# Channel attention with a squared-ReLU feed-forward: q's first loads on a second queue, W's low terms and v's split in another order, the last block stored in three pieces

## The chip, the cores and the metric

One core of one Trainium2 chip runs the kernel. The metric is the device time of one execution in microseconds (us), taken as the median of the runs shown; less is better. One execution was also recorded by the hardware profiler, and all rows below are of that execution.

## What is computed

Four batches of q, k and v (6080 tokens x 256 channels, f32) go through attention over the channels, and the result, read as 24320 tokens of 256 channels, through a feed-forward layer:

```python
qn = q / (norm(q, axis=1) + 1e-6);  kn = k / (norm(k, axis=1) + 1e-6)
s = kn.T @ qn / tau                      # 256 x 256 per batch
a = softmax(s, axis=-1)
x = (v @ a).reshape(24320, 256)
h = maximum(x @ w_in, 0)                 # 2048 wide
return (h * h) @ w_out
```

w_in and w_out come as 64-bit floats. The kernel gets v and gives the output with the channels first.

## The kernel before, in words

**What is multiplied.** The kernel never forms x. For each batch it makes a matrix W from a and w_in (256 x 2048), and then for each block of tokens h = relu(v W), and the output from h squared and w_out. All big products are made from two halves of 32 bits that TensorE takes in one pass: a value is split into `hi` and `lo`, and a product is three terms, hi by hi, lo by hi and hi by lo. A batch has 12 blocks of tokens, ten of 512 and two of 480; a block has 16 steps f of 128 hidden channels. One step is a first product (L579: six matmuls into a `ps_h` bank, then ScalarE's Relu into `x`), and two steps later a second product (L629) into `ps_o`. Between them, once for each pair of steps, ScalarE squares `x` (L603), copies it to `g_hi`, and VectorE makes `g_lo` (L616). Most blocks use a scheme with seven products in place of eight for a pair (L651), the first two blocks and the very last one the plain eight (L707).

**The start (batch 0).** `start_first` (L310) walks over the 25 chunks of q and k: 23 of two rows for each partition, one of a single row, one of the last 64 tokens. `load(c)` asks for a chunk nine ahead, k and q as one DMA each of 256 KB, all from the SP queue (L267, L268); chunk 0 is asked for in two halves. Before these the SP queue asks for `tau` (L106), and ScalarE runs one small `first` activation (L113). TensorE multiplies each chunk into `gram` in plain f32, ScalarE squares it, VectorE adds the squares to `acc`. `LAST = 1` chunk is left for later: its products come from `rest` (L347), after the sums of squares.

**From the gram matrix to W.** `softmax_and_W` (L407) is a generator that the loop at L771 moves on, one yield at a time; `beside_first` (L758) names what is put between. In order: the sums of squares over the partitions (`ps_n`), a chain of small VectorE operations to `nr`, the matrices `diag` and `s`, `ps_b`, the softmax, the transposes `ps_t`, the halves of its transpose `eT_hi` and `eT_lo`, and W's products `ps_w`. For group g of 512 columns of W, `products(h, terms)` makes for half h term 0 (wi_hi by eT_hi), term 1 (wi_hi by eT_lo) and term 2 (wi_lo by eT_hi); `evict(h)` copies `ps_w` to `w_hi` (ScalarE) and `w_lo` (VectorE). Meanwhile TensorE makes gram products of the next batch from its first `HEAD = 6` chunks ("heads", plain f32, L355); the other chunks of batches 1 to 3 are split and multiplied with three terms beside the steps (L384).

**The first steps.** The loop at L798 goes over the steps. In the first 32 of them (two blocks, group by group) other work is put between by hand: `stages` (L778) moves on the decoding of the weights from 64-bit floats (item 2 becomes w_in's group 1 with `wi_hi` and `wi_lo`, and so on), `steps_of_W` (L782) names the steps 6, 14 and 22 in which the next group of W is made, and `split_v_lo` (L566) makes `v_lo` of the second block in step 1, after the step's stages. Every instruction of TensorE, VectorE and ScalarE is kept in the order in which it is written (L19), so all of these have the line L27 in the profile.

**The end.** The last block's two halves m of the output lie in one `ps_o` tile of two banks. The last step does the matmuls of m = 0 first (L717). Then ScalarE copies m = 0 and VectorE m = 1 into one tile `o`, and each half is stored from the SP queue (L741).

Of the kernel before, what the change touches and what calls it, by code (L numbers as in the profile page):

```python
# [8 lines left out]
F32 = mybir.dt.float32  # L9
# [21 lines left out]
def kernel(  # L31
# [21 lines left out]
    nc = tc.nc  # L53
# [12 lines left out]
    J = 2  # L66
    NPAIR = NF // 2
    PPG = FPG // 2
    LAST = 1


    NB = -(-N // T)
# [30 lines left out]
    ones = const.tile([P, P], F32, name="ones")  # L103
    vector.memset(ones, 1.0)
    tau_sb = const.tile([P, 1], F32, name="tau_sb")
    nc.sync.dma_start(tau_sb, tau.to_broadcast([P, 1]))  # L106

    exp_bias = const.tile([P, 1], F32, name="exp_bias")
    vector.memset(exp_bias, -896.0 * 2.0**23)

    for _ in range(7):
        tensor.matmul(ps_h.tile([P, T], F32, tag="h", name="ps_first")[:, 0:P], ones, ones, start=True, stop=True)
    scalar.activation(const.tile([P, 1], F32, name="first"), exp_bias, AF.Square)  # L113
    wo_hi = const.tile([P, NF, C], F32R, name="wo_hi")
    wo_lo = const.tile([P, NF, C], F32R, name="wo_lo")
    late = {}
# [119 lines left out]

    W = {}
    now = {"part": 0}
    HEAD = 6
    QK_BUFS = 2  # L240
    FAST_TAGS = ("qk",) * QK_BUFS + ("w_lo",) * NG + ("w_hi",) * NG

    class Gram:
# [14 lines left out]
        def load(self, c, tag="qk", raw=None):  # L258
            p, jn, _ = self.q[c]
            if raw is None:  # L260
                at = pool if tag == "qk" else wpool
                bufs = dict(bufs=QK_BUFS) if tag == "qk" else {}
                raw = at.tile([P, 2, J, C], F32, tag=tag, name=f"qk{self.b}_{c}", **bufs)

            pieces = [(j, j + 1) for j in range(jn)] if self.b == 0 and c == 0 else [(0, jn)]
            for j0, j1 in pieces:
                nc.sync.dma_start(raw[:p, 1, j0:j1, :], self.k[c][2][:, j0:j1, :])  # L267
                nc.sync.dma_start(raw[:p, 0, j0:j1, :], self.q[c][2][:, j0:j1, :])  # L268
            self.raws[c] = raw

        def products(self, c, parts):
# [38 lines left out]
    def start_first(b=0):  # L310

        g = grams[0] = Gram(0)
        total = g.n + HEAD
        AHEAD = len(FAST_TAGS) - 1

        ROOM = 4
        room = pool.tile([P, ROOM, 2, J, C], F32, tag="wS_lo", name="qk_heads", bufs=1)

        def load(c):
            if c == g.n:  # L320
                grams[1] = Gram(1)
            if c < g.n:
                g.load(c, FAST_TAGS[c % len(FAST_TAGS)])
            elif c < total and B > 1:
                grams[1].load(c - g.n, raw=room[:, c - g.n] if c - g.n < ROOM else None)

        for c in range(AHEAD):
            load(c)
        for c in range(g.n):
            if c < g.n - LAST:  # L330
                for _ in g.products(c, [(g.raws[c], g.raws[c])]):
                    pass
            g.squares(c)
            if c:
                g.add_squares(c - 1)
            load(c + AHEAD)
            if c in (2, 15):
                weights.load(int(c > 2))
            if c in (13, 14, 15, 17):
                weights.stage(0)  # L340
            if c == 19:
                load_v(*order[0])
        for c in range(g.n + AHEAD, total):
            load(c)
        g.add_squares(g.n - 1)

        def rest():  # L347
            for c in range(g.n - LAST, g.n):
                for _ in g.products(c, [(g.raws[c], g.raws[c])]):
                    pass  # L350
            yield

        return rest()
# [53 lines left out]
    def softmax_and_W(b):  # L407
# [81 lines left out]
        for g in range(NG):  # L489
            while (b, g) not in may_write_W:  # L490
                yield
            if b == 0:
                while g not in wi_first:
                    yield
                hi, lo = wi_first.pop(g)
                keep_w_in(g, (hi, lo))
            else:
                hi, lo = wi.pop(g)
            w_hi = wpool.tile([P, NC, GRP], F32R, tag="w_hi", name=f"w_hi{b}_{g}")
            w_lo = wpool.tile([P, NC, GRP], F32R, tag="w_lo", name=f"w_lo{b}_{g}")  # L500
            ps_w = {}

            def products(h, terms=range(3)):
                if h not in ps_w:
                    ps_w[h] = ps_h.tile([P, T], F32, tag="h", name=f"ps_w{b}_{g}_{h}")
                for i in terms:
                    et, wt = ((eT_hi, hi), (eT_lo, hi), (eT_hi, lo))[i]
                    for d in range(NC):
                        tensor.matmul(
                            ps_w[h][:, 0:GRP],  # L510
                            et[:, d, h * P : (h + 1) * P],
                            wt[:, d, :],
                            start=i == 0 and d == 0,
                            stop=i == 2 and d == NC - 1,
                        )

            def evict(h):
                ps = ps_w.pop(h)[:, 0:GRP]
                scalar.activation(w_hi[:, h, :], ps, AF.Copy, scale=rinv[:, h : h + 1])
                vector.scalar_tensor_tensor(  # L520
                    w_lo[:, h, :],
                    ps,
                    rinv[:, h : h + 1],
                    w_hi[:, h, :].bitcast(F32),
                    op0=ALU.mult,
                    op1=ALU.subtract,
                )

            if b == 0:
                for h, terms in ((0, (0, 1)), (1, (0,)), (0, (2,)), (1, (1, 2))):  # L530
                    products(h, terms)
                yield
                for h in range(NC):
                    evict(h)
            else:
                for h in range(NC):
                    products(h)
                    if h == NC - 1 and g + 1 < NG:
                        wi[g + 1] = reload_w_in(b, g + 1)
                    yield  # L540
                    evict(h)
                    yield
            W[b, g] = w_hi, w_lo
            yield
# [162 lines left out]
    def eight_products(b, n, r, part):  # L707
        t0, tn = blocks[n]
        f = 2 * r + part
        if f == 0:  # L710
            O[b, n] = ps_acc.tile([P, NC, T], F32, tag="o", name=f"ps_o{b}_{n}")
        hi, lo = (x.rearrange("p s t -> p (s t)")[:, part * tn : (part + 1) * tn] for x in G[b, n, r])
        parts = ((wo_hi, hi), (wo_lo, hi), (wo_hi, lo))
        order_of = [(i, m) for i in range(3) for m in range(NC)]
        last = (b, n, f) == steps[-1]
        if last:
            order_of.sort(key=lambda im: im[1])  # L717
        for i, m in order_of:
            wt, gt = parts[i]
            tensor.matmul(  # L720
                O[b, n][:, m, :tn],
                wt[:, f, m * P : (m + 1) * P],
                gt,
                start=f == 0 and i == 0,
                stop=f == NF - 1 and i == 2,
            )
        if part:
            del G[b, n, r]
        if f == NF - 1:
            o = pool.tile([P, NC, tn], F32, tag="o_sb", name=f"o{b}_{n}", bufs=1)  # L730
            at = b * N + t0
            out = outT[:, at : at + tn].rearrange("(m p) t -> p m t", p=P)
            psum = O.pop((b, n))
            for m in range(NC):
                ps = psum[:, m, :]
                if last and m:
                    vector.tensor_copy(o[:, m, :], ps[:, :tn])
                else:
                    scalar.copy(o[:, m, :], ps[:, :tn])
                if last:  # L740
                    nc.sync.dma_start(out[:, m : m + 1, :], o[:, m : m + 1, :])  # L741
            if not last:
                nc.sync.dma_start(out, o)

    steps = [(0, n, g * FPG + f) for g in range(NG) for n in range(min(2, NB)) for f in range(FPG)]
    PAIR = len(steps)
# [10 lines left out]

    beside_first = {  # L758
        1: (lambda: next(rest), stage(1), lambda: load_v(*order[1], "acc")),
        5: (head, head, head, head, stage(0), stage(1)),  # L760
        6: (lambda: split_v_hi(*order[0]),),
        8: (head, head, head, head),
        9: (stage(0),),
# [34 lines left out]
    for i in range(len(steps) + 2 * LAG):  # L798
# [8 lines left out]
        if i >= PAIR:  # L807
            gens = (beside,)
        else:
            for item in stages.get(i, ()):  # L810
                weights.stage(item)
            if i == 1:
                split_v_lo(*order[1])
            gens = (first,) if i in steps_of_W else ()
            if i >= 16 and (i >= 24 or part == 0):
                gens += (squares_of_heads if B > 1 and grams[1].raws else sums,)
# [5 lines left out]
                next(gen, None)  # L822
        if part == 0 and 0 <= i // 2 - 1 < len(pairs):
            parts_of_sums(*pairs[i // 2 - 1])
        if i in steps_of_W:
            next(first)
        if part == 1 and i // 2 < len(pairs):
            squares_and_sums(*pairs[i // 2])
        if part and late_work:
# [4 lines left out]
                pass  # L834
        if i >= 2 * LAG:
            second_product(*pairs[i // 2 - LAG], part)
        if i < len(steps):
            at_hi, at_lo = (None, None) if at == 0 else (12, 13) if at == 1 else (6, 8)
            if i == 2 and len(order) > 2:
# [37 lines left out]
```

## Time and profile before

| what | us |
|---|---|
| median of 3 runs | 2215.76 (2215.72 to 2216.32) |
| the profiled execution, its own time | 2216.45 |
| its span on the core | 2214.6 |
| TensorE busy in the span | 2206.4 |
| ScalarE busy | 1842.3 |
| VectorE busy | 1759.8 |

The span is what the rows show, from the first instruction to the last; the execution's own time is 1.85 us more, and lies 0.69 us above the median of the runs. PE is TensorE's matmuls, PEld its weight loads, which run beside the matmuls; DVE is VectorE, ACT ScalarE, SPq the queue that issues DMAs. An f32 matmul shows as two records. In the timeline a row has its start and its length in us, then engine, line, operation, out<-in, the shape, how many are merged (x), and in brackets the idle time before it with what ended it.

### The profile page before, as it was taken

What the parts mean: (1) busy time and instruction counts of PE and PEld (TensorE: products, weight loads), DVE (VectorE), ACT (ScalarE), POOL (GpSimd) and SP (SyncE); (2) the same over time, 40 slices, a digit from 0 to 9 for tenths busy, and PEclk for the clock granted to TensorE, in tenths of its full rate; (3) what the DMA queues carried; (4) which work ended last, traced back from release to release, by engine and by line L of the source; (5) the groups of instructions that cost most, each with busy time, mean ns of one, the idle gap of its engine ahead of it and who ended that gap; (6) DMA issues with size and microseconds to landing.
All of it is one profiled execution on the core that took longest, in us unless ns stands there. A gap on an engine that the chain in (4) does not pass through costs nothing.

```text
span 2214.6 us, 34388 instructions
## 1 busy us (share of the span) xinstructions
PE 2206.4 (100%) x13750; PEld 1982.2 (90%) x13750; DVE 1759.8 (79%) x2469; ACT 1842.3 (83%) x2294; POOL 0.7 (0%) x6
## 2 busy tenths in 40 slices
PE   9999999999999999999999999999999999999999
PEld 8788999989989999998998999998899888888898
DVE  6878888888778888878767888888877777777773
ACT  5788888888788888888878888888887888888885
POOL 0000000000000000000000000000000000000000
PEclk9999999999999999999999999999999999999999
DMA  9521122101111122110121222110102010010000
GB/s 342 179 77 38 60 75 67 46 19 38 57 67 58 61 70 70 55 41 22 36 76 48 69 64 69 58 53 23 37 20 76 21 37 20 22 36 20 22 26 18
DMA packets 76496, 127.01 MB, mean 57 GB/s; under 512 B 7728, under 2 KB 35120, under 8 KB 76336
## 3 DMA queue, kind: packets, MB, share of 16 engines
q1 hardware_dynamic: 76336, 124.81, 17.3%
q8 instruction: 108, 1.77, 0.3%
q14 instruction: 52, 0.43, 0.1%
HBM read 95.68 MB, written 29.10 MB: 56 GB/s over the span
## 4 chain that ended last, share of the span: by engine, by line
PE 98%; DVE 1%; DMA 0%; ACT 0%; issue 0%; SPq 0%; DVEq 0%
PE ps_h L27 47%; PE ps_o L27 43%; PE gram L27 6%; PE ps_w L27 2%; DVE dec_m L27 0%; DMA qk<-in_q 0%; DMA w_raw<-in_w_in 0%; PE ps_n L27 0%; DVE wi_lo L27 0%; ACT x L27 0%; ACT g_hi L27 0%; DVE w_lo L27 0%; PE ps_t L27 0%; PE ps_b L27 0%; DVE g_lo L27 0%
## 5 line engine op out<-in xcount | busy, mean ns | idle before, releaser
L27 DVE TENSOR_TENSOR g_lo<-x,g_hi 128x768 fp32r<-128x768 f32 (+2 forms) x744 | 804.2, 1081 | 97.2 <-ACT g_hi L27 96.5
L27 DVE TENSOR_TENSOR x<-x 128x256 f32<-128x256 f32 (+3 forms) x1080 | 550.8, 510 | 274.5 <-ACT x L27 249.1
L27 ACT CAST g_hi<-x 128x768 fp32r<-128x768 f32 (+2 forms) x744 | 697.8, 938 | 25.0 <-DVE x L27 12.2
L27 ACT ACTIVATE x<-ps_h 128x512 f32<-128x512 f32 (+1 forms) x768 | 455.7, 593 | 289.7 <-PE ps_h L27 266.0
L27 PE MATMUL ps_h<-v_hi,w_hi 128*128 128x512 f32 (+1 forms) x1536 | 478.5, 393 | 0.0
L27 PE MATMUL ps_h<-v_hi,w_lo 128*128 128x512 f32 (+1 forms) x1536 | 477.8, 392 | 0.0
L27 PE MATMUL ps_h<-v_lo,w_hi 128*128 128x512 f32 (+1 forms) x1536 | 475.0, 390 | 0.8 <-DVE v_lo L27 0.8
L27 ACT ACTIVATE x<-x 128x1024 f32<-128x1024 f32 (+1 forms) x384 | 404.4, 1053 | 11.9
L27 PE MATMUL ps_o<-g_lo,wS_hi 128*128 128x256 f32 (+1 forms) x1440 | 401.9, 279 | 0.0
L27 PE MATMUL ps_o<-g_hi,wS_lo 128*128 128x256 f32 (+1 forms) x1440 | 401.2, 279 | 0.0
L27 PE MATMUL ps_o<-g_hi,wS_hi 128*128 128x256 f32 (+1 forms) x1440 | 400.4, 278 | 0.0
L27 PEld LDWEIGHTS ps_h<-v_lo,w_hi 128*128 128x128 f32 x1536 | 287.8, 187 | 65.9 <-DVE v_lo L27 1.2
L27 PEld LDWEIGHTS ps_h<-v_hi,w_lo 128*128 128x128 f32 x1536 | 288.5, 188 | 62.4 <-DVE w_lo L27 0.3
L27 PE MATMUL ps_o<-g_hi,wo_hi 128*128 128x256 f32 (+3 forms) x1176 | 330.9, 288 | 0.0
L27 PE MATMUL ps_o<-g_hi,wo_lo 128*128 128x256 f32 (+3 forms) x1176 | 330.7, 288 | 0.0
L27 PE MATMUL ps_o<-g_lo,wo_hi 128*128 128x256 f32 (+3 forms) x1176 | 330.5, 288 | 0.0
L27 PEld LDWEIGHTS ps_o<-g_lo,wS_hi 128*128 128x128 f32 x1440 | 271.0, 188 | 15.9 <-DVE g_lo L27 0.2
L27 PEld LDWEIGHTS ps_o<-g_hi,wS_hi 128*128 128x128 f32 x1440 | 270.3, 188 | 15.5
L27 PEld LDWEIGHTS ps_o<-g_hi,wS_lo 128*128 128x128 f32 x1440 | 270.6, 188 | 0.0
L27 PEld LDWEIGHTS ps_h<-v_hi,w_hi 128*128 128x128 f32 x1536 | 238.9, 188 | 5.3
L27 PEld LDWEIGHTS ps_o<-g_hi,wo_hi 128*128 128x128 f32 x1176 | 221.5, 188 | 16.4
L27 PEld LDWEIGHTS ps_o<-g_lo,wo_hi 128*128 128x128 f32 x1176 | 220.8, 188 | 16.6 <-DVE g_lo L27 0.3
(90 smaller groups left out, 1668.1 us busy)
## 6 DMA issues: line engine op xcount, KB each, us to landing
qk<-in_k SPq DMA_DIRECT2D x87, 256.0 KB, 2.7
qk<-in_q SPq DMA_DIRECT2D x87, 256.0 KB, 3.0
v<-in_vT SPq DMA_DIRECT2D x40, 512.0 KB, 3.7
out_T<-o SPq DMA_DIRECT2D x152, 128.0 KB, 1.7
wi_hi<-wi_kept SPq DMA_DIRECT2D x12, 512.0 KB, 3.3
wi_lo<-wi_kept SPq DMA_DIRECT2D x12, 512.0 KB, 4.1
w_raw<-in_w_in SPq DMA_DIRECT2D x4, 1024.0 KB, 5.7
w_raw<-in_w_out SPq DMA_DIRECT2D x4, 1024.0 KB, 5.2
```

The costliest lines, as they stand in the source:

```text
L27: return lambda *args, **kwargs: self.tc.keep_in_program_order(issue(*args, **kwargs))
```

## The change

- q's pieces of chunks 0 to 3 of batch 0 are asked for from ScalarE's queue; `tau` and the `first` activation come after the nine chunks that are loaded ahead.
- `LAST` is 2 and `HEAD` is 5; in place 5 of `beside_first` two heads are run instead of four.
- W of batch 0: terms 0 and 1 of both halves come first, then a yield, then term 2 of both and the copies. In the steps of W the second `next(first)` comes after the step's second product.
- In step 1 `v_lo` of the second block is made before the step's stages.
- The last block has one `ps_o` tile for each half. Half 0 is copied by ScalarE and stored from SP; half 1 is copied in two pieces, one by VectorE (stored from SP) and one by ScalarE (stored from ScalarE's queue), each into a tile of its own.

```diff
-    LAST = 1
+    LAST = 2
...
     tau_sb = const.tile([P, 1], F32, name="tau_sb")
-    nc.sync.dma_start(tau_sb, tau.to_broadcast([P, 1]))
...
-    scalar.activation(const.tile([P, 1], F32, name="first"), exp_bias, AF.Square)
...
-    HEAD = 6
+    HEAD = 5
...
             pieces = [(j, j + 1) for j in range(jn)] if self.b == 0 and c == 0 else [(0, jn)]
+
+            other = scalar if self.b == 0 and c < 4 else nc.sync
             for j0, j1 in pieces:
                 nc.sync.dma_start(raw[:p, 1, j0:j1, :], self.k[c][2][:, j0:j1, :])
-                nc.sync.dma_start(raw[:p, 0, j0:j1, :], self.q[c][2][:, j0:j1, :])
+                other.dma_start(raw[:p, 0, j0:j1, :], self.q[c][2][:, j0:j1, :])
...
         for c in range(AHEAD):
             load(c)
+        nc.sync.dma_start(tau_sb, tau.to_broadcast([P, 1]))
+        scalar.activation(const.tile([P, 1], F32, name="first"), exp_bias, AF.Square)
...
             if b == 0:
-                for h, terms in ((0, (0, 1)), (1, (0,)), (0, (2,)), (1, (1, 2))):
+                for h, terms in ((0, (0, 1)), (1, (0, 1))):
                     products(h, terms)
                 yield
+                for h in range(NC):
+                    products(h, (2,))
                 for h in range(NC):
                     evict(h)
...
+        final = (b, n) == order[-1]
         if f == 0:
-            O[b, n] = ps_acc.tile([P, NC, T], F32, tag="o", name=f"ps_o{b}_{n}")
+
+            tiles = [
+                ps_acc.tile([P, NC, T], F32, tag="o", name=f"ps_o{b}_{n}_{i}") for i in range(NC if final else 1)
+            ]
+            O[b, n] = [tiles[m % len(tiles)][:, m, :tn] for m in range(NC)]
...
-        last = (b, n, f) == steps[-1]
+        last = final and f == NF - 1
...
+            if last:
+                half = tn // 2
+                for tag, m, t, copy, queue in (
+                    ("acc", 0, slice(0, tn), scalar.copy, nc.sync),
+                    ("dec", 1, slice(0, half), vector.tensor_copy, nc.sync),
+                    ("o_sb", 1, slice(half, tn), scalar.copy, scalar),
+                ):
+                    o = pool.tile([P, t.stop - t.start], F32, tag=tag, name=f"o{b}_{n}_{tag}", bufs=1)
+                    copy(o, psum[m][:, t])
+                    queue.dma_start(out[:, m, t], o)
+                return
...
-        5: (head, head, head, head, stage(0), stage(1)),
+        5: (head, head, stage(0), stage(1)),
...
+            if i == 1:
+                split_v_lo(*order[1])
             for item in stages.get(i, ()):
                 weights.stage(item)
-            if i == 1:
-                split_v_lo(*order[1])
...
-        if i in steps_of_W:
-            next(first)
...
         if i >= 2 * LAG:
             second_product(*pairs[i // 2 - LAG], part)
+        if i in steps_of_W:
+            next(first)
```

## Rows read from the trace of the kernel before

**Rows 1.** The page: busy time of the engines, the chain's shares.

```profile
PE 2206.4 (100%) x13750; PEld 1982.2 (90%) x13750; DVE 1759.8 (79%) x2469; ACT 1842.3 (83%) x2294; POOL 0.7 (0%) x6
...
PE 98%; DVE 1%; DMA 0%; ACT 0%; issue 0%; SPq 0%; DVEq 0%
```

**Rows 2.** Timeline of the first 9 us: SP's queue, ScalarE, weight loads.

```profile
0.73 1.28 ACT L27 ACT_TABLE_LOAD   x1 [0.73 <-PEq L867]
0.74 0.38 SPq L106 DMA_DIRECT2D tau_sb<-in_tau  x1
...
1.18 0.42 SPq L267 DMA_DIRECT2D qk<-in_k  x1
...
5.88 0.97 PEld L27 LDWEIGHTS gram<-qk 128*128 128x128 f32 x4 [0.19 <-issue]
...
8.70 21.45 PEld L27 LDWEIGHTS gram<-qk 128*128 128x128 f32 x100 [1.85 <-issue]
```

**Rows 3.** The chain that ended last, in order of time: start, length, what.

```profile
3.54 5.05 DMA qk<-in_q
8.73 39.09 PE gram L27 x180
```

**Rows 4.** The DMA view of 0 to 9 us: 40 slices, the sum.

```profile
GB/s 0 0 0 0 0 0 0 0 0 19 37 101 128 187 373 337 351 237 159 118 96 205 278 355 373 346 337 373 382 373 337 301 237 228 155 264 346 355 310 319
DMA packets 1415, 1.80 MB, mean 200 GB/s; under 512 B 279, under 2 KB 791, under 8 KB 1415
```

**Rows 5.** Timeline of 27 to 48 us, VectorE's sums of squares and TensorE's ps_n.

```profile
27.36 1.23 DVE L27 TENSOR_TENSOR acc<-acc,sq 128x1024 f32<-128x1024 f32 x1 [2.81 <-ACT sq L27]
...
45.70 0.69 DVE L27 TENSOR_TENSOR acc<-acc 128x512 f32<-128x512 f32 x1
...
47.44 1.08 PEld L27 LDWEIGHTS ps_n<-ones,acc 128*128 128x128 f32 x8
```

**Rows 6.** Timeline of 49 to 54 us, from ps_n to ps_b.

```profile
49.59 3.32 PEld L27 LDWEIGHTS gram<-qk_heads 128*128 128x128 f32 x16 [0.33 <-issue]
...
51.96 0.48 DVE L27 TENSOR_SCALAR diag<-ident,nr 128x128 f32<-128x128 f32 x2
...
52.93 0.41 PEld L27 LDWEIGHTS ps_b<-diag,ones 128*128 128x128 f32 x2
```

**Rows 7.** Timeline of 58 to 63 us, W's first group.

```profile
58.47 0.30 PEld L27 LDWEIGHTS ps_w<-wi_hi,eT_hi 128*128 128x128 f32 x2 [0.38 <-issue]
...
60.27 0.30 PEld L27 LDWEIGHTS ps_w<-wi_lo,eT_hi 128*128 128x128 f32 x2 [0.37 <-DVE wi_lo L27]
...
61.96 0.69 ACT L27 ACTIVATE w_hi<-ps_w,rinv 128x512 fp32r<-128x512 f32 x1 [0.23 <-PE ps_w L27]
```

**Rows 8.** Timeline of 68 to 72 us, v_lo of the second block and g_hi.

```profile
68.47 1.22 DVE L27 TENSOR_TENSOR v_lo<-v,v_hi 128x1024 fp32r<-128x1024 f32 x1
...
69.74 0.30 PEld L27 LDWEIGHTS ps_h<-v_lo,w_hi 128*128 128x128 f32 x2 [1.21 <-DVE v_lo L27]
...
71.09 1.03 ACT L27 CAST g_hi<-x 128x1024 fp32r<-128x1024 f32 x1
```

**Rows 9.** Busy time in one stretch (columns: length, PE, PEld, DVE, ACT).

```profile
66.20:72.10 5.90, 5.12 (x24) 3.95 (x23) 4.62 (x5) 5.87 (x8) 0.00 (x0) 1.00 0.53 173
```

**Rows 10.** Timeline at 80 us, W's second group.

```profile
80.26 0.30 PEld L27 LDWEIGHTS ps_w<-wi_lo,eT_hi 128*128 128x128 f32 x2 [0.97 <-DVE wi_lo L27]
```

**Rows 11.** Weight loads at 195 us: six gram matmuls of a split chunk, then ps_h.

```profile
195.63 0.19 PEld L27 LDWEIGHTS gram<-qk_hi 128*128 128x128 f32 x1
...
196.35 0.31 PEld L27 LDWEIGHTS ps_h<-v_hi,w_hi 128*128 128x128 f32 x2
```

**Rows 12.** Timeline of the end.

```profile
2210.33 0.56 ACT L27 COPY o<-ps_o 128x480 f32<-128x480 f32 x1 [3.94 <-PE ps_o L27]
2210.92 1.02 SPq L741 DMA_DIRECT2D out_T<-o  x2
2210.93 0.66 DVE L27 COPY o<-ps_o 128x480 f32<-128x480 f32 x1 [3.34 <-ACT o L27]
```

More of the change, by code (lines that the diff above doesn't have):

```diff
@@ L720, in eight_products @@
             tensor.matmul(
-                O[b, n][:, m, :tn],
+                O[b, n][m],
                 wt[:, f, m * P : (m + 1) * P],
@@ L729, in eight_products @@
         if f == NF - 1:
-            o = pool.tile([P, NC, tn], F32, tag="o_sb", name=f"o{b}_{n}", bufs=1)
             at = b * N + t0
@@ L733, in eight_products @@
             psum = O.pop((b, n))
-            for m in range(NC):
[L735 to L743, printed above, removed]
+            if last:
[9 more added lines that the diff above has]
+                return
+            o = pool.tile([P, NC, tn], F32, tag="o_sb", name=f"o{b}_{n}", bufs=1)
+            for m in range(NC):
+                scalar.copy(o[:, m, :], psum[m])
+            nc.sync.dma_start(out, o)
     steps = [(0, n, g * FPG + f) for g in range(NG) for n in range(min(2, NB)) for f in range(FPG)]
```

## The prediction

> **What bounds the kernel now.** I read the page first. TensorE is busy 2206.4 of 2214.6 us, and the chain that ended last is TensorE for 98% [rows 1]. So time can come from three places only: the stretch before TensorE is packed, the tail after its last matmul, and matmuls added or taken away in between. The timeline of the first 9 us and the chain in order of time show the first: TensorE has chunk 0, then stands until q's part of chunk 1, asked for at 3.54, has landed 5.05 us later [rows 2, 3]; from 8.73 the gram products follow without a gap. The timeline then shows who ends each later wait: ps_b is late because of TensorE itself [rows 6], W's first group waits for wi_lo [rows 7], the second block for v_lo [rows 8], W's second group for wi_lo [rows 10]. After 80.3 nothing waits until the tail, where two copies run one after the other [rows 12].
>
> The sum below is made against the profiled execution: 2216.45 us, of which 2214.6 are its span. It is 0.69 above the median of the runs, 2215.76; I take the same difference off that median.
>
> **The start.** tau's issue leaves the front: k goes at 0.74 in place of 1.18 [rows 2], a gain of 0.44. SP issues at a pitch of some 0.47 (1.18 to 3.54 is five issues). q on ScalarE's queue runs beside it: q's half pieces at 0.73 and 1.20, chunk 1 at 1.67 in place of 3.54. With the same 5.05 to land it is there at 6.7. TensorE's four loads of chunk 0's second half begin at 5.88 and end at 6.85 [rows 2]; the next could follow at 6.87 and came at 8.70, so 1.83 of waiting goes, and 0.1 ahead of chunk 0. LAST = 2 takes chunk 23, two f32 matmuls or four records, from before ps_n to after it: at 0.216 a record (16 in 3.32 plus a pitch, [rows 6]) 0.86. TensorE would reach ps_n at 47.44 - 1.9 - 0.86 = 44.7 [rows 5].
>
> But ps_n also needs the sum of squares, which VectorE ends at 45.70 + 0.69 = 46.39, in a chain packed since 27.36, where it waited 2.81 for a square that waited for its chunk [rows 5]. This chain moves by what the stream of loads moves. No row shows that, so bounds: at least tau's 0.44. At most: 1.80 MB had moved by 9.0 [rows 4]; a stream that starts 0.44 earlier (transfers first show in slice 11, at 2.5, so 2.04) and at once runs at the 380 GB/s of the best slices would have moved 6.96 x 0.38 = 2.6 MB, 0.8 more, or 2.1 us. Slices 17 to 20, starved by the issues, should fill; the dip of slices 31 to 35, with much in flight, may stay. I take 1.5, nearer the upper bound because most of the deficit is in the starved slices. Then acc is ready at 44.9, later than TensorE, and ps_n starts there: **-2.5** (bounds -1.3, where tau's 0.44 is all and TensorE comes to ps_n at 46.1, and -2.76).
>
> Here the Trainium skill speaks against the change. Its page "DMA: Bandwidth & Descriptors", section "Issuing engines are not separate DMA queues", says that loads issued by several engines run on the same DMA engines, and that only the issuing time is saved, usually small beside the transfer. The first half agrees with the trace; the second does not, since an issue of 0.47 is more than the 0.34 that 128 KB take at 380 GB/s. By the rule alone the start would be worth little over tau's part, the first rival below.
>
> ScalarE's new work: five issues at the same pitch, to 3.1, then the table load of 1.28 [rows 2] and `first`, 4.6 in all. Even with 1 us of waiting between the issues the first square can start before chunk 0's last piece was there before (5.88, when TensorE took it up [rows 2]); nothing is lost. SP's queue is moved past tau only.
>
> **ps_n to W.** Before, VectorE's chain had diag ready at 51.96 + 0.48 = 52.44, and TensorE, still in the heads, came to ps_b at 52.93 [rows 6]. Now 8 records of `rest` and 8 of heads lie there in place of 4 and 16: 3.5 us and the gap of 0.33, less than the chain's 5.0 from ps_n. ps_b follows diag: **-0.44**.
>
> W's first group: the head's four records now come ahead of term 2. The wait of 0.37 for wi_lo [rows 7] goes, but the head no longer lies beside the copies. Before, w_hi of half 1 began 61.96 - 58.47 = 3.49 after ps_w. Now 8 records (1.9, with the wait for eT_lo), the head (0.86) and four more (0.93) put the last matmul's result near 3.9 and the copies of 0.69 behind it, about 0.5 later, with only the loss of the wait to set against it. VectorE's w_lo, and the decoding queued behind it, come some 0.4 later: **+0.4** (bounds 0 and +0.7, a whole copy).
>
> **The first steps.** v_lo moved ahead of the other VectorE operation of step 1, 1.14 at pitch, ends TensorE's wait: it could start at 68.77 and came at 69.74 [rows 8]. I cost this gain of 0.97 at **0**: the second product behind it needs g_hi, which ScalarE begins at 71.09, and ScalarE is busy 5.87 of 5.90 us there [rows 9]. TensorE arrives earlier and waits for g_hi and g_lo instead. wo_lo becomes 1.14 later and is needed only with them. If that cover fails, the term is -0.97.
>
> W's second group: TensorE waits 0.97 in its load queue for wi_lo, about 0.92 over the usual pitch [rows 10]. With the second product (six records, 1.39) ahead of term 2 it is hidden; the copies come later but are needed two steps on, some 5.5 us: **-0.92** (bounds 0 and -0.92). Groups 2 and 3 show no such wait.
>
> **HEAD = 5.** Chunk 5 of batch 1 leaves the heads (that is in ps_b's term) and becomes a split chunk: 12 matmuls beside batch 1's work, at (196.35 - 195.63) / 6 = 0.12 each [rows 11], **+1.42**, in full, because TensorE has no idle time there [rows 1]. Bounds: 0 if small gaps take it, 2.4 if it cost VectorE's two passes of 1.22 instead. Its load moves out of the first rush; nothing waits for it.
>
> **The tail.** Half 0 need not wait for half 1, and is off the path. Half 1's VectorE copy of 240 columns begins with the last matmul, at 2210.33 where ScalarE's began [rows 12]; between 0.33 and 0.66, I take 0.41. Its ScalarE piece lies in the same tile and bank. Before, VectorE's copy waited for ScalarE's, 3.34 idle and released by it [rows 12], although they read two halves of one tile. So I let the pieces follow each other: 2210.78, plus 0.36 (scaled from 0.56), the store issued at 2211.18, against 2210.92 + 1.02 - 0.33 = 2211.61: **-0.43**; side by side it would be -0.85. The Trainium skill's page "PSUM — Partial Sum Buffer", section "PSUM bank collisions raise a hardware error", says that two engines must not access one bank in the same partitions at the same time, two reads included. By that rule, too, the sum has -0.43 here and not -0.85. The second `ps_o` tile waits for the copy of the block before, done just as it is needed: under 0.1.
>
> **Sum.** -2.5 - 0.44 + 0.4 + 0 - 0.92 + 1.42 - 0.43 = -2.5: a span of 2212.1, and 2215.76 - 2.5 = **2213.3**.
>
> **Rivals.**
> - The start saves tau's part only, since the DMA engines, not the issues, set the landing: ps_n -1.3 (0.44, and LAST's 0.86), the sum -1.27: 2214.5. For it: slices of 340 to 380 follow soon [rows 4]. Against: the starved slices 17 to 20. It is what the Trainium skill's section on issuing engines, named above, would have.
> - Everything pays: the start -2.76, v_lo -0.97, the split chunk in gaps for 0, the tail -0.85. Sum -5.5: 2210.3. Against: ScalarE's 5.87 of 5.90 [rows 9], and a TensorE without gaps.
> - Slower: q on the second queue lands late, behind the table load and with its share of the engines halved by SP's longer queue. With no gain at the start but LAST's 0.86 the sum is -0.86 - 0.44 + 0.4 - 0.92 + 1.42 - 0.43 = -0.83. So it decides once chunk 1 reaches TensorE later than 8.73 + 0.83 = 9.6, and each us beyond costs one. At 10.6 it gives 2216.8. Against: even with the table load ahead, q's chunk 1 goes at 1.67 + 1.28 = 2.95, before the old 3.54.
> - That the change doesn't do what it says would be tau or q still issued in the old place; that is the first rival's time or 2215.8.
>
> **How the numbers follow.** The forecast's case, with its own bounds some 2212.4 to 2214.2, has 0.70, the first rival 0.14, the second 0.12, the third 0.04. The range reaches into the first and the second rival: 2211.3 to 2215.2. 0.2%, 4.4 us, is about what a measurement of this kernel can tell from no change. Faster by more than that is the second rival: 0.12. Slower by more would need chunk 1 at 14: 0.02. The rest, 0.86, is within.
>
> **What would show it.** The first load of chunk 1 near 6.9; ps_n near 44.9, with VectorE's acc just ahead; ps_b right behind diag; no wait for wi_lo, but ps_h waiting for w_hi; no wait for v_lo at the second block, but one for g_hi or g_lo; no wait at W's second group; 12 more split gram matmuls and 8 f32 records fewer; in the tail the last store issued from ScalarE near 0.85 after the last matmul's copy could begin. It is wrong if the stretch to W's second group shrinks by under 2 or over 4.5 us, or if batch 1 grows by nothing, or by over 2.

## The result, and the profile after

The changed kernel takes 2219.79 us (median of 17 runs, 2218.54 to 2222.94), the kernel before 2216.34 (17 runs, 2215.16 to 2218.44): a ratio of 1.0018, interval 1.0011 to 1.0026. The forecast was 2213.3 and its range ended at 2215.2. Four of the 17 runs, 2221.9 and more, show a granted clock of 0.998 or 0.999, of which more below. The profiled execution took 2219.3 us, its span is 2217.5, 2.9 longer than before.

The page: TensorE is as packed as in [rows 1], with four records more, and DMA now has 1% of the chain.

```profile
PE 2208.8 (100%) x13754; PEld 1982.3 (89%) x13754; DVE 1761.1 (79%) x2470; ACT 1843.8 (83%) x2296; POOL 0.7 (0%) x6
...
PE 97%; DVE 1%; DMA 1%; ACT 1%; issue 0%; SPq 0%; DVEq 0%; ACTq 0%
```

The timeline of the first 9 us, beside [rows 2, 3]:

```profile
0.74 3.21 ACTq L27 DMA_DIRECT2D qk<-in_q  x5
0.74 3.88 SPq L267 DMA_DIRECT2D qk<-in_k  x6
...
4.66 0.89 SPq L268 DMA_DIRECT2D qk<-in_q  x1
5.27 0.20 ACT L27 ACTIVATE first<-exp_bias 128x1 f32<-128x1 f32 x1
...
8.16 0.33 SPq L267 DMA_DIRECT2D qk<-in_k  x1
...
8.19 1.56 PE L27 MATMUL gram<-qk 128*128 128x256 f32 x6 [1.67 <-DMA qk<-in_q]
```

All is asked for earlier, as meant, but chunk 1 reaches TensorE at 8.19 in place of 8.73, not at 6.9. The DMA view of 0 to 9 us, beside [rows 4], says why:

```profile
DMA  0000000175699999978397949469898989999999
GB/s 0 0 0 0 0 0 0 23 64 105 182 373 351 360 378 383 305 264 200 146 200 182 209 164 209 146 219 228 319 337 346 382 328 319 337 401 410 428 401 373
DMA packets 1400, 2.04 MB, mean 227 GB/s; under 512 B 148, under 2 KB 660, under 8 KB 1400
...
qk<-in_q ACTq DMA_DIRECT2D x3, 256.0 KB, 7.3
```

The slow slices are still there (146 to 264 GB/s in slices 17 to 27, counted from 0 as in the prediction), while more is in flight and the DMA engines are mostly busy (first line, tenths). The same line of the kernel before, which stands above the rates of [rows 4], has 5 to 8 tenths in the slices 17 to 20 that the prediction called starved:

```profile
DMA  0000000003548599975867899999999989579989
```

By 9 us 0.24 MB more has moved than before, not the 0.8 of the upper bound, and a piece of q takes 7.3 us to land, in place of 5.5. Behind 9 us even this lead goes. The DMA view of 9 to 20 us, the kernel before and the changed one:

```profile
DMA packets 2359, 4.30 MB, mean 391 GB/s; under 512 B 261, under 2 KB 261, under 8 KB 2359
DMA packets 2268, 3.87 MB, mean 352 GB/s; under 512 B 377, under 2 KB 377, under 8 KB 2268
```

This is so in every trace. The six with q on the second queue (after, e1, e3, e4, e8, e9) move 2.00 to 2.22 MB up to 9 us and 3.54 to 4.17 from there to 20 us; the eleven others move 1.72 to 1.90 and 4.25 to 4.41. Why the stream is slower there is not shown. In the changed kernel the square that VectorE's sums wait for comes later for it, beside the 27.36 of [rows 5]:

```profile
27.86 1.23 DVE L27 TENSOR_TENSOR acc<-acc,sq 128x1024 f32<-128x1024 f32 x1 [3.55 <-ACT sq L27]
```

The timeline of 44 to 54 us, beside [rows 5, 6]: TensorE now waits ahead of ps_n for VectorE's sums, which are ready at 46.91 (46.39 before), and ps_b comes right behind diag.

```profile
46.22 0.69 DVE L27 TENSOR_TENSOR acc<-acc 128x512 f32<-128x512 f32 x1
...
47.05 1.02 PE L27 MATMUL ps_n<-ones,acc 128*128 128x1 f32 x8 [0.62 <-DVE acc L27]
47.94 2.17 PE L27 MATMUL gram<-qk 128*128 128x256 f32 x8
...
50.04 1.99 PE L27 MATMUL gram<-qk_heads 128*128 128x256 f32 x8
...
51.44 0.48 DVE L27 TENSOR_SCALAR diag<-ident,nr 128x128 f32<-128x128 f32 x2
...
52.08 0.67 PE L27 MATMUL ps_b<-diag,ones 128*128 128x256 f32 x2
```

W and the first steps, beside [rows 7, 8, 10]: ps_h waits for w_hi, the wait for v_lo has become one for g_hi, and at 80.92 nothing waits for wi_lo.

```profile
61.92 1.08 PE L27 MATMUL ps_h<-v_hi,w_hi 128*128 128x512 f32 x2 [0.31 <-ACT w_hi L27]
...
71.68 0.73 PE L27 MATMUL ps_o<-g_hi,wo_hi 128*128 128x512 f32 x2 [0.49 <-ACT g_hi L27]
...
80.46 0.62 PE L27 MATMUL ps_o<-g_lo,wo_hi 128*128 128x512 f32 x2
80.92 1.09 PE L27 MATMUL ps_w<-wi_lo,eT_hi 128*128 128x512 f32 x4
```

The tail, beside [rows 12]: half 1's two pieces follow each other, and ScalarE's is released by VectorE's.

```profile
2213.32 0.38 PE L27 MATMUL ps_o<-g_lo,wo_hi 128*128 128x480 f32 x1
...
2213.74 0.41 DVE L27 COPY o_dec<-ps_o 128x240 f32<-128x240 f32 x1 [2.69 <-PE ps_o L27]
...
2214.18 0.36 ACT L27 COPY o_o_sb<-ps_o 128x240 f32<-128x240 f32 x1 [0.53 <-DVE o_dec L27]
2214.57 0.35 ACTq L27 DMA_DIRECT2D out_T<-o_o_sb  x1
```

The last matmul of the kernel before:

```profile
2209.91 0.38 PE L27 MATMUL ps_o<-g_lo,wo_hi 128*128 128x480 f32 x1
```

From the last matmul's start to the end of the span: 2217.5 - 2213.3 = 4.2, before 2214.6 - 2209.9 = 4.7.

**Where the time went.** I took the start of the same matmul in both traces, after less before: ps_b -1.06, first ps_h -0.52, the step at 84 us **-1.30**, then 157.8 us -0.59, 608 us +1.88, 1701 us +2.38, the last matmul **+3.40**. The matmul at 84 us, before and after:

```profile
84.55 0.63 PE L27 MATMUL ps_o<-g_hi,wo_hi 128*128 128x512 f32 x2
83.24 0.63 PE L27 MATMUL ps_o<-g_hi,wo_hi 128*128 128x512 f32 x2
```

So the early part gained, 1.3 in place of the forecast 3.5, and 4.7 were lost where the change put only 12 matmuls. The loss has no wait in it but one (0.6 for qk_lo). Beside this wait and the 12 matmuls, the same matmuls simply follow at a longer pitch, that is, with more time from one start to the next. VectorE makes v_lo once for each block, so its first and last start in batch 3 tell a block's length. The kernel before, that tile's line for 1740 to 2140 us:

```profile
L27 DVE TENSOR_TENSOR v_lo<-v,v_hi x9: 1151/1219/1220, 1772.8 to 2107.7; 128x1024 fp32r<-128x1024 f32 x8, 128x960 fp32r<-128x960 f32 x1
```

The changed kernel:

```profile
L27 DVE TENSOR_TENSOR v_lo<-v,v_hi x9: 1150/1219/1221, 1775.2 to 2111.0; 128x1024 fp32r<-128x1024 f32 x8, 128x960 fp32r<-128x960 f32 x1
```

Eight blocks take 334.9 and 335.8 us: 41.86 and 41.98 each, for the same instructions in the same order. Two things in the built programs differ there: the order in which the three banks of `ps_h` are taken, and the place of wo_hi and wo_lo in SBUF. The one-column tile of the `first` activation is allocated where its instruction is written; before, it lay ahead of them, now behind, and they stand 32 bytes lower (17600 and 33984 in place of 17632 and 34016).

### The profile page after: what moved, and what is told of

It is laid out like the page before. It is cut to its first block, busy times and chain, and to the rows that moved or that the text cites. A ratio compares the mean times of both kernels' runs of the same rounds, so it can differ in the third digit from the quotient of the medians.

```text
span 2217.5 us, 34392 instructions
## 1 busy us (share of the span) xinstructions
PE 2208.8 (100%) x13754; PEld 1982.3 (89%) x13754; DVE 1761.1 (79%) x2470; ACT 1843.8 (83%) x2296; POOL 0.7 (0%) x6
## 4 chain that ended last, share of the span: by engine, by line
PE 97%; DVE 1%; DMA 1%; ACT 1%; issue 0%; SPq 0%; DVEq 0%; ACTq 0%
PE ps_h L27 47%; PE ps_o L27 42%; PE gram L27 5%; PE ps_w L27 2%; DMA qk<-in_q 1%; DVE acc L27 1%; ACT x L27 0%; PE ps_n L27 0%; DVE dec_m L27 0%; DVE g_lo L27 0%; DVE x L27 0%; ACT sq L27 0%; ACT dec_m L27 0%; PE ps_b L27 0%; ACT g_hi L27 0%
```

## Experiments on the pitch

**e1 and e2: the banks.** PSUM tiles of `ps_h` get three tags of one buffer, taken in turn (e1: step -1 in the changed kernel; e2: step 1 in the kernel before).

```diff
+        self.at = (self.at + self.step) % 3
+        return self.pool.tile(shape, dtype, tag=f"h{self.at}", name=name)
```

> The changed kernel, with the bank of every ps_h, ps_w and small PSUM tile chosen by hand: the three banks are taken in descending order (6, 5, 4), as they were in the kernel before, where the changed kernel takes them in ascending order (4, 5, 6). Nothing else differs. Comparing the two traces, the same matmuls of the steps follow each other at a longer pitch in the changed kernel: 233 ns in place of 228 for 512 columns from 86 to 158 us, and 41.97 in place of 41.87 us for each block of batch 3, some 2.3 us in all, with no wait. Theory banks: the order of the banks sets the pitch; blocks of batch 3 go back to 41.87 us and the time to about 2217.5. Theory address: wo_hi and wo_lo stand 32 bytes lower in SBUF; nothing changes here, 2219.8. Theory instructions: the pitch hangs on the program's own place in memory or on the chip; nothing changes, 2219.8 within 1.

> The kernel before, with the three banks taken by hand in ascending order. Theory banks: blocks of batch 3 grow to 41.97 us and the time to about 2218.6. Theories address and instructions: as the kernel before, 2216.3 and 41.87 within 0.02.

Measured: 2272.51 and 2266.43 us. The fixed turn brings waits of its own around W (ps_w for w_lo, 14.1 us in either, and some 19 us of ps_h), and a granted clock of 0.991 to 0.995, so the times say nothing. The blocks of batch 3 do: matched matmul by matmul, 0.106 longer than before in e1, unchanged within 0.001 in e2. Each keeps the pitch of its wo place, whichever way the banks turn. Theory banks falls, and e3 below says the same: there one small allocation is moved, the banks turn as in the changed kernel, and the pitch is the old one.

**e3, e5, e6, e11: the place.** e3 is the changed kernel, e5, e6 and e11 are the kernel before, with only allocations moved.

```diff
 e3
     tau_sb = const.tile([P, 1], F32, name="tau_sb")
+    first_sb = const.tile([P, 1], F32, name="first")
 e5: wo_hi, wo_lo ahead of first; e6: ahead of exp_bias
-    scalar.activation(const.tile([P, 1], F32, name="first"), exp_bias, AF.Square)
     wo_hi = const.tile([P, NF, C], F32R, name="wo_hi")
     wo_lo = const.tile([P, NF, C], F32R, name="wo_lo")
+    scalar.activation(const.tile([P, 1], F32, name="first"), exp_bias, AF.Square)
 e11
-const.tile([P, 1], F32, name="first")
+const.tile([P, 16], F32, name="first")[:, 0:1]
```

> The changed kernel, with the one-column tile of the first activation allocated where the kernel before has it (its instruction stays in its new place), so that wo_hi and wo_lo are at the SBUF addresses of the kernel before again (17632 and 34016 in place of 17600 and 33984). Theory address: 2217.5 and blocks of batch 3 at 41.87 us. Theories banks and instructions: 2219.8, blocks at 41.97.

> The kernel before with one thing changed: wo_hi and wo_lo are allocated ahead of the tile of the first activation, so they stand 32 bytes lower (17600 and 33984), as in the changed kernel. No instruction is moved. Theory address: the pitch of the changed kernel appears here: blocks of batch 3 at 41.97 us in place of 41.87, 86 to 158 us 0.7 longer, the last matmul about 2.3 later, the time about 2218.3. Rival, the pitch comes from something else that the changed kernel with wo at its old place also lost: 2216.0 and 41.87.

> The kernel before with wo_hi and wo_lo 64 bytes lower (17568 and 33952), all else in place but three one-column tiles. Theory that the place within 64 bytes counts: 17568 has the same as 17632, so blocks of batch 3 stay at 41.87 us and the time at 2216.0. Rival, any other place has its own pitch: blocks differ from 41.87 by more than 0.02.

> The kernel before with the tile of the first activation 64 bytes long: wo_hi, wo_lo and every tile behind them in SBUF stand 32 bytes higher (wo_hi 17664, w_hi of group 0 66816, g_hi 200224). Theory that the place of one tile against another counts: blocks of batch 3 stay at 41.87 us. Theory that a tile's own place counts: the pitch changes, in either direction, by up to 0.2 us for a block.

Measured: e5 and e6 2218.12 us each beside 2215.88 for the kernel before on that chip, **+2.24**, one run of each; e11 2215.36, one run, beside 2216.31 (21 runs); e3 2219.0, for in six of its 11 runs the clock fell (below), and the five others have the middle 2216.86, where the changed kernel's 13 at clock 1.0 have 2219.69. The v_lo line of e3:

```profile
L27 DVE TENSOR_TENSOR v_lo<-v,v_hi x9: 1150/1217/1217, 1773.7 to 2108.6; 128x1024 fp32r<-128x1024 f32 x8, 128x960 fp32r<-128x960 f32 x1
```

e6:

```profile
L27 DVE TENSOR_TENSOR v_lo<-v,v_hi x9: 1155/1220/1221, 1773.3 to 2109.1; 128x1024 fp32r<-128x1024 f32 x8, 128x960 fp32r<-128x960 f32 x1
```

e11:

```profile
L27 DVE TENSOR_TENSOR v_lo<-v,v_hi x9: 1149/1222/1222, 1771.8 to 2106.7; 128x1024 fp32r<-128x1024 f32 x8, 128x960 fp32r<-128x960 f32 x1
```

334.9, 335.8 and 334.9 us for eight blocks; e5 has 335.7 (1773.6 to 2109.3). So the change with wo at its old place has the old pitch, and the kernel before with wo 32 or 64 bytes lower has the new one: the cause is shown from both sides. By matched matmuls the lower place costs 2.4 and 2.5 us behind ps_n in e5 and e6, and 2.6 between e3 and the changed kernel. It is not spread evenly: of e5's 2.4, 0.56 fall between 84 and 158 us, 0.83 from there to 1701, 1.03 behind. The rule of 64 bytes falls with e6. In e11 wo, w, v and g all moved by the same 32 bytes and nothing changed, so it is the place of one tile against the others that counts. Which tiles, and in what way, is not settled.

**e12 and e13: another place.** The kernel of e10 (below: the tail and W's groups 1 to 3 of the change, on the kernel before), with wo_hi and wo_lo ahead of all constants.

```diff
+    wo_hi = const.tile([P, NF, C], F32R, name="wo_hi")
+    wo_lo = const.tile([P, NF, C], F32R, name="wo_lo")
     ident = const.tile([P, P], F32, name="ident")
```

> The kernel with the tail and W's groups 1 to 3 alone (2214.9 in the run before this), with wo_hi and wo_lo allocated ahead of every other constant: 1120 bytes lower against all tiles of the steps (16512 in place of 17632). The places 32 and 64 bytes lower both gave blocks of 41.97 us in batch 3. Theory, the old place is a good one among many worse: blocks above 41.87, a time of 2215 to 2218. Rival, only places just below the old one are bad: 41.87 and 2215. A gain, blocks below 41.80, would show that the old place was not the best either.

> The same kernel as in the run before (tail, W's groups 1 to 3, wo_hi and wo_lo ahead of all other constants), now timed against the kernel before. Its one trace had blocks with 12 split gram matmuls 0.115 us shorter, blocks of batch 3 unchanged, 0.5 lost from 84 to 158 us. Theory, the pitch is fixed by the place: 2214.9 - 1.2 to 1.7, so 2213.2 to 2213.9, and the same block times. Rival, the gain was chance: 2214.9.

Measured: 2213.92 once, then **2213.41** (11 runs, 2213.18 to 2213.68) beside 2215.93 (27 runs): 0.9989, interval 0.9980 to 0.9997. It beats both kernels. e10's v_lo line for 640 to 1690 us, batches 1 and 2:

```profile
L27 DVE TENSOR_TENSOR v_lo<-v,v_hi x23: 1150/1216/1221, 683.6 to 1680.9; 128x1024 fp32r<-128x1024 f32 x19, 128x960 fp32r<-128x960 f32 x4
```

e13's:

```profile
L27 DVE TENSOR_TENSOR v_lo<-v,v_hi x23: 1150/1217/1221, 683.7 to 1679.7; 128x1024 fp32r<-128x1024 f32 x19, 128x960 fp32r<-128x960 f32 x4
```

997.3 against 996.0, in the blocks with gram matmuls; blocks without them take 41.87 in both. The old place was a good one, not the best.

## Experiments on LAST, HEAD and the clock

**e4, e14, e15, e9.** e4 is the changed kernel with HEAD = 6 and four heads; e14 and e15 are the kernel before with LAST = 2, and with HEAD = 5 and two heads; e9 is the change with neither, wo at its old place.

```diff
 e14
-    LAST = 1
+    LAST = 2
 e15 (e4 undoes this in the changed kernel, e9 this and LAST)
-    HEAD = 6
+    HEAD = 5
-        5: (head, head, head, head, stage(0), stage(1)),
+        5: (head, head, stage(0), stage(1)),
```

> The changed kernel with HEAD = 6 and four heads in place 5 again, so that chunk 5 of batch 1 is multiplied in plain f32 in the heads and not split. By the records, the 12 extra split matmuls cost 1.45 beside batch 1 and one wait of 0.73 behind them; four f32 records of 0.216 come back ahead of ps_b (0.86), where the chain of small operations hides some or all. Theory full price: 2219.8 - 1.45 - 0.73 + 0 to 0.86, so 2217.6 to 2218.5. Rival, the gram matmuls fill idle slots: 2219.8 or more.

> The kernel before with LAST = 2 alone. Theory: ps_n is set by VectorE's sums, so nothing is saved ahead of it (0 to 0.2); TensorE stands idle there 0.2 to 0.9 us, and the four records of chunk 23 come between ps_n and ps_b, where 4 + 16 records already cover VectorE's chain: ps_b 0.7 to 0.86 later, the time about 2216.9, and a run with 0.998 (3 to 4 us more) now and then. Rival: the idle time is not what the clock falls by; all runs at 1.0 within 1.5 us.

> The kernel before with HEAD = 5 and two heads in place 5. Theory: beside batch 1 12 more split matmuls and one wait for qk_lo cost 2.1; ahead, ps_b comes 0.5 earlier (right behind diag, with TensorE idle 1.5 to 2 us ahead of it) and the other eight records less save nothing where VectorE sets the pace: 2216.2 + 1.4 to 1.7, with a fall of the clock behind the idle time in some runs. Rival, the eight f32 records saved (1.7) pay for it: 2216.2 to 2216.7, all at 1.0.

> The changed kernel with wo_hi and wo_lo at their old place (the tile of the first activation allocated where it was), LAST = 1, HEAD = 6 and four heads in place 5: the start, the moves and the tail of the change together. Without LAST = 2 TensorE comes to ps_n as late as VectorE's sums and does not stand idle ahead of it. Theory: the fall of the granted clock behind ps_n (0.5 from 48.9 to 55 us in one trace, 0.998 of the run) comes with that idle time, so no run here shows it, and the runs agree within 1.5 us; the time is 0.2 (moves) + 0.5 (tail) + 0 to 0.3 (start) below the kernel before, 0.7 to 1.0. Rival: the fall comes from the start (other loads, other issue) or from chance; then one run in three still shows 0.998 and 3 to 4 us more.

Measured: e4 2219.16 (11 runs) beside 2215.88; e14 2217.90 (10 runs, 2215.85 to 2220.38) and e15 2217.41 (10 runs, 2216.94 to 2218.40) beside 2215.93 (27 runs, 2215.20 to 2216.55); e9 2215.50 (11 runs) beside 2216.31, 0.9996, interval 0.9987 to 1.0005.

In e4 ps_b has 8 records of `rest` and 16 of the heads ahead of it, and its 2219.16 is no gain that these runs can tell: 3.3 over the kernel before, as the whole change 3.45. The full price that was expected back is not seen in the time. In the traces it does come back where it was paid: from 158 to 608 us e4 is 2.15 shorter than the changed kernel. It is spent again ahead of ps_b: e14, with the same records there and no fall of the clock in its trace, takes 6.54 us from ps_n to ps_b, the changed kernel 5.03.

```profile
46.66 1.02 PE L27 MATMUL ps_n<-ones,acc 128*128 128x1 f32 x8
...
53.20 0.59 PE L27 MATMUL ps_b<-diag,ones 128*128 128x256 f32 x2
```

HEAD alone (e15) costs 1.48: a ratio of 1.0007, whose interval, 0.9998 to 1.0017, takes in 1, but all ten runs lie above the longest of the 27 before. Its trace: ps_b follows diag, with TensorE idle ahead of it, and that saves 0.48 from ps_n to ps_b (5.01 after 5.49). The kernel before, then e15:

```profile
47.65 0.95 PE L27 MATMUL ps_n<-ones,acc 128*128 128x1 f32 x8
...
49.59 3.72 PE L27 MATMUL gram<-qk_heads 128*128 128x256 f32 x16
...
53.14 0.59 PE L27 MATMUL ps_b<-diag,ones 128*128 128x256 f32 x2
```

```profile
47.97 1.02 PE L27 MATMUL ps_n<-ones,acc 128*128 128x1 f32 x8
...
52.98 0.67 PE L27 MATMUL ps_b<-diag,ones 128*128 128x256 f32 x2 [1.01 <-DVE diag L27]
```

From 158 to 608 us e15 loses 2.10, by matched matmuls: 12 more of 0.12, and a wait which is in the waits of e15 and of the changed kernel, and not in those of the kernel before:

```profile
PE gram L27 <- DVE qk_lo L27: 0.6, 1, 0.6
```

LAST alone (e14) saves nothing by ps_b, which starts at 53.20 where it was 53.14: ps_n is 0.99 earlier, within the spread of its start (below), and the records that left its front lie behind it. The runs fall into two lots: five at clock 1.0, 2215.85 to 2217.16, and five at 0.998 or 0.999, 2218.65 to 2220.38. So do those of e3 (five of 11 at 2216.01 to 2217.08, six at 2219.0 to 2221.58) and of e4 (six of 11 at 2218.48 to 2219.16, five at 2220.33 to 2222.43). Without LAST the fall is rare: in e9 and in e10 one of 11 runs shows 0.999 and is the longest, 2217.18 and 2217.15; in e15 one of 10 shows it, and that one is no longer than the rest; in e13 none does; of the 71 runs of the kernel before beside e1 to e15 four show 0.999 and none 0.998. e4's profile caught the fall. Its windows (after the length: PE, PEld, DVE, ACT, POOL, then the granted clock):

```profile
47.00:48.00 1.00, 0.80 (x8) 0.83 (x8) 1.00 (x3) 0.00 (x0) 0.00 (x0) 1.00 1.05 397
48.00:49.00 1.00, 1.00 (x6) 0.74 (x6) 0.89 (x5) 0.00 (x0) 0.00 (x0) 0.87 1.06 393
49.00:50.00 1.00, 1.00 (x3) 0.50 (x2) 0.83 (x6) 0.00 (x0) 0.00 (x0) 0.50 1.05 389
...
55.00:56.00 1.00, 1.00 (x5) 0.85 (x4) 0.00 (x0) 0.00 (x0) 0.00 (x0) 0.72 0.88 291
```

And its timeline:

```profile
47.20 1.02 PE L27 MATMUL ps_n<-ones,acc 128*128 128x1 f32 x8 [1.02 <-DVE acc L27]
48.08 3.42 PE L27 MATMUL gram<-qk 128*128 128x256 f32 x8
51.44 5.75 PE L27 MATMUL gram<-qk_heads 128*128 128x256 f32 x16
57.02 0.59 PE L27 MATMUL ps_b<-diag,ones 128*128 128x256 f32 x2
```

TensorE stood 1.02 us ahead of ps_n, ran its one-column matmuls, and then had half its clock, 1.2 of 2.4 GHz, until past 55 us. The 8 records of `rest` took 3.36 from start to start in place of 2.10, the 16 of the heads 5.58 in place of the 3.55 of [rows 6], as the starts of the matmuls give it: 3.3 us. With 0.62 of standing in the profile of the changed kernel, 0.75 in e1's and 0.82 in e3's, the clock stayed there. That LAST brings the fall is shown (e14 beside the kernel before); that the standing ahead of ps_n is what does it fits all runs, but no run changed it alone, and e15's 1.01 ahead of ps_b brought none.

The traces of e1 and e2 bear on it, since e2 has no LAST = 2. Every fall in them before the end stands by a wait of TensorE of 1.85 us or more, as this one of e2:

```profile
455.86 0.50 PE L27 MATMUL ps_h<-v_hi,w_hi 128*128 128x512 f32 x1 [3.58 <-DVE nx L27]
```

Its granted clock was 0.50 in the window from 457 to 458 us and 1.00 in that from 460 to 461. But not every such wait has a fall behind it: one of 1.88 us at 600 us of e1 has, the same one at 595 us of e2 has none. So standing is seen to bring the fall in some runs and not in others.

## Experiments on the start, the moves and the tail

**e7, e8, e10.** All on the kernel before: e7 has the moves in W, of v_lo and of `next(first)` and the tail, as in the change's diff; e8 its start alone; e10 the tail and, for groups 1 to 3 only, the moves in W:

```diff
+                if g:
+                    for h in range(NC):
+                        products(h, (0, 1))
+                else:
+                    for h, terms in ((0, (0, 1)), (1, (0,)), (0, (2,)), (1, (1, 2))):
+                        products(h, terms)
                 yield
+                if g:
+                    for h in range(NC):
+                        products(h, (2,))
```

> The kernel before with the moves behind the start and the tail of the change, without q's second queue, tau's and the first activation's move, LAST and HEAD; wo stays at its place. By the prediction: the first ps_h 0.4 later, nothing for v_lo, 0.92 saved at W's second group, 0.43 saved in the tail: a span 0.95 shorter. By the trace of the changed kernel: first ps_h 0.47 later, +0.1 at the next steps, 0.9 saved at 80 us, which lasts (no loss at groups 2 and 3), 0.51 saved in the tail: a span 0.85 to 0.95 shorter. Rival: the gain at 80 us is given back at W's next groups, where term 2 and the copies come later than before; then only the tail's 0.5 less the 0.5 of the first group, so no change.

> The kernel before with the start of the change alone: q's pieces of chunks 0 to 3 from ScalarE's queue, tau and the first activation behind the nine chunks; LAST = 1 and HEAD = 6 stay, wo stays at its place. By the prediction: chunk 1 at 6.9 us, ps_n 1.9 earlier (45.5), ps_b 1.2 or more earlier. By the trace of the changed kernel the DMA engines set the landing: chunk 1 at about 8.2, ps_n 0.5 earlier, no idle TensorE ahead of it and no fall of the clock, and a span 0.3 to 0.6 shorter.

> The kernel before with two things alone: the tail of the change, and in W's groups 1 to 3 of batch 0 terms 0 and 1 first, then the yield, then term 2 and the copies, with the second call behind the step's second product. Group 0 keeps its old order; v_lo, the start, LAST and HEAD stay. By the trace with all moves (0.77 saved at 80 us, 0.58 lost at group 0, 0.52 saved in the tail) the loss of group 0 goes: 0.7 to 0.8 + 0.5 below the kernel before, a span of 2212.8 to 2213.0 where before has 2214.1 on this chip, ratio 0.9994. Rival: the 0.77 is given back when group 0 is faster; then the tail's 0.5 alone.

Measured: e7 2215.28 and e8 2216.12 beside 2215.88, one run each; e10 2214.94 (11 runs) beside 2216.31 (21 runs), 0.9994, interval 0.9985 to 1.0003, not to be told from 1 by itself.

e7 against the trace of before, matched matmuls: W's first group loses 0.58; the second block starts 0.93 earlier and has given it back when the second product comes; group 1 of W gains 0.77, which stays; 0.52 less from the last matmul to the end. Together -0.7, near the first theory's -0.95. e10 keeps the 0.78 and loses nothing at group 0.

e8's gain is not there. Its ps_n starts at 47.35, but that start moves by itself. With the loads as before and LAST = 1 it is 47.65, 47.0, 47.0, 46.95, 47.35, 46.9, 46.7, 47.55, 46.9 and 48.0 (before, e2, e5, e6, e7, e10 to e13, e15), a mean of 47.2; e12 and e13 are the same kernel. With q on the second queue and LAST = 1 it is 47.35 and 47.5 (e8, e9). With LAST = 2 it is 46.7 with the loads as before (e14), and 47.05, 46.5, 47.1 and 47.2 with the second queue (after, e1, e3, e4). In e9, where it is timed with the moves and the tail, the whole gain of 0.8, itself not to be told from 0, is covered by those two.

## Why the forecast was wrong

By the parts measured alone: wo's place +2.24, HEAD +1.48, LAST +0.4 where the clock stays (2216.33, the middle of its five, against 2215.93), the moves -0.2, the tail -0.5, the start 0: +3.4, and +3.45 was measured. Each part carries some tenths (LAST's five runs span 1.3), and HEAD and LAST share the stretch ahead of ps_b, so an agreement this close is luck. The forecast was -2.5, so 5.9 are to be explained: the start with LAST 2.9, the place of wo 2.2, HEAD with ps_b 0.5, the moves 0.3.

By its own signs the prediction was wrong twice: the stretch to W's second group shrank by 1.3, under 2, and batch 1 grew by 2.1 (e15) to 2.5 (the changed kernel), over 2.

- **The place of wo** was in no step. The sum let `first` cost nothing but its time on ScalarE, "4.6 in all", and did not see that its tile is allocated on the same line. None of the rivals had it. Without it the change would still be some 1.2 slower.
- **The start, -2.5, is the step that failed,** and the largest part of the miss. "Slices 17 to 20, starved by the issues, should fill" was wrong: such slices stay with twice the issuing, so the issues were not what slowed them, and from 9 to 20 us 0.43 MB less moved than before. acc was ready at 46.9, not 44.9, chunk 1 there at 8.2, not 6.7. What does set the rate of the loads there stays open. (A slip beside it: [rows 4] has the first transfers in slice 9, at 2.0 us, not in slice 11.) The first rival had the mechanism; even tau's 0.44 can't be found in ps_n's spread of 0.9 to 1.3. I had weighed the Trainium skill ("DMA: Bandwidth & Descriptors", "Issuing engines are not separate DMA queues": DMAs of all engines share the same DMA engines, so only issuing time is saved) against the row of an issue of 0.47, and followed the row. The trace of before could not agree with the first half, as the prediction says, for all its loads are on one queue; and 128 KB took 2.8 us to land there, not the 0.34 of the best rate, so the issue is the small part after all. The traces agree with that section of the Trainium skill: ScalarE's queue saved the issuing, and a transfer took 7.3 us in place of 5.5.
- **LAST's 0.86** was saved on TensorE and in good part stood idle there (0.62 in the changed kernel), since VectorE's sums set ps_n. The prediction had the sums end later than TensorE, and did not ask what an idle TensorE does to its clock.
- **HEAD, +1.42,** was mis-sized: 2.1, since the split chunk also brings a wait of 0.6 for qk_lo. ps_b right behind diag, -0.44, held (0.48 in e15).
- **W's first group, +0.4:** 0.58, in its bounds. **v_lo, 0:** right, with the cover that was named, g_hi. **W's second group, -0.92:** 0.77 to 0.81 (e7, e9, e10, e3, the changed kernel).
- **The tail, -0.43:** 0.51, the pieces one behind the other. Here the row and the Trainium skill ("PSUM — Partial Sum Buffer", "PSUM bank collisions raise a hardware error") had said the same. ScalarE's piece is released by VectorE's in the tail's rows, which shows that they are kept in order, not what the chip would do without it.

## What to carry to other kernels

Where one engine is packed end to end, compare the pitch of the same instructions in both traces before looking for waits, and look at the SBUF addresses: an edit that moves a line with an allocation in it moves tiles. Work taken off the front of a packed engine is worth nothing where another engine's sum ends later, and TensorE, left standing there, lost its clock too in 20 of the 49 runs with LAST = 2. Time each part of a bundle alone: here two parts paid (0.5 and 0.8 us), and the bundle hid them.

## What the runs showed of the hardware that I had not expected

- 32 or 64 bytes in the place of a weights' tile against the other tiles change the pitch of matmuls by 0.26% (41.87 to 41.98 us a block of 264 matmuls in batch 3), the same in all five traces with the lower place (after, e1, e4, e5, e6), with no wait in the profile of these blocks.
- One wait of 1.02 us ahead of eight one-column matmuls was followed by some 7 us at half the clock (e4), which cost 3.3 us.
- The start of ps_n, behind 47 us of loads, differs by 0.6 us between two traces of one kernel (e12, e13) and by 0.9 between nine traces with the same loads (1.3 with e15, which has one chunk less in its heads), as much as the early terms that were measured.
- Loads issued from two queues in place of one moved more by 9 us (2.00 to 2.22 MB after 1.72 to 1.90) and less from 9 to 20 us (3.54 to 4.17 after 4.25 to 4.41), in all 17 traces.
